# Agent attention and a maxout feed-forward in one kernel: the sum of exponentials folded on GpSimd at batch borders, with other orders around them and other engines for the last tiles

## Chip, cores and metric

The kernel runs on one core of a Trainium2 chip. Its time is the device time of one execution in microseconds; the time before is the median of six runs. Lower is better. The engines are named as in the profile: PE is TensorE (PEld its weight loads), DVE is VectorE, ACT is ScalarE, POOL is GpSimd, SP issues most of the DMAs.

## What is computed

There are 4 batches of 12544 tokens with 128 channels, 49 agents per batch, and a feed-forward with 768 hidden columns. Inputs and output are float32.

```python
def _attn_ref(q, k, v, agents):
    scale = 1.0 / np.sqrt(q.shape[-1])
    def sm(a, b):
        s = scale * (a @ b.transpose(0, 2, 1))
        s = s - s.max(-1, keepdims=True)
        e = np.exp(s)
        return e / (e.sum(-1, keepdims=True) + 1e-09)
    agent_v = sm(agents, k) @ v
    return sm(q, agents) @ agent_v

def _moe_ref(x, w1, w2, w3, w_out):
    h = np.maximum(np.maximum(x @ w1, x @ w2), x @ w3)
    return h @ w_out
```

The second function is applied to the rows that the first returns.

## The kernel before

**What it does with the algebra.** For each batch the 49 agents' values are formed from all of k and v. Their products with the differences w3-w1 and w2-w1 (and, for hidden block 4, with w3-w2) and with w1 @ w_out are kept in a tile G, one per batch. A token then needs only its 49 exponentials e: u = e·G(first difference), relu, v = e·G(second difference), a maximum, the product of the result with w_out, plus a linear term from G. The division by the sum of a token's exponentials comes last, on the output.

**Groups.** The tokens of q are worked off in 49 groups of 1024 (s = 0 to 48). Groups 0 to 11 are batch 0, 12 to 23 batch 1, 24 to 35 batch 2, 36 to 47 batch 3. Group 48 takes the last 256 tokens of each batch, so its u and v come in 8 matmuls of 128 columns instead of 2 of 512. A group has these steps; a step is named with its hidden block (0 to 5) or its half of the group (0 or 1), and with its group where that matters:

- qt, qe: q turned on PE (L651, 8 matmuls), copied to SBUF on DVE (L655). From group 36 on, and at groups 12, 24 and 36, a transposing DMA does this instead (L659).
- s, ex: scores (L665, 64-column matmuls) and exponentials e_q on ACT (L671).
- sum, rec: sums of the exponentials on PE (L676), their reciprocals on DVE (L682).
- u0 to u5, a0 to a5: first hidden product (L688, matmuls with 49 rows, two at a time) and relu on ACT (L703; block 4 in place, L700).
- v0 to v5, x0 to x5: second product (L688) and the maximum on DVE (L713; block 4 as a relu on ACT, L711). v4 adds onto the PSUM tile of u4, so it needs a4.
- lin0, lin1: linear term of each half (L718, 2 matmuls). oc00 to oc05, oc10 to oc15: output product of each half and block (L727, 4 matmuls of 128 columns each). sc0, sc1: division on DVE (L734). st: the output DMA on SP (L741).

u and v tiles (2 banks each) share a ring of three PSUM buffers; each is returned by its a or x (u4's by x4). Scores, sums, q's and the output halves share two single banks.

**The next batch beside it.** While the q groups of batch b-1 run, k and v of batch b are taken in 11 portions of 9 tiles of 128 rows (the last of 8), one per group: loads on SP, casts on POOL (L515, L519), k turned by a DMA (L523), scores ks (L366), exponentials ke on ACT (L371), values kv on PE (L535) and ka on DVE (L540). The step ea (L547, first portion L551) adds the exponentials of the first ten portions, 128x441 in float32, into Eacc on POOL.

**The border.** At groups 11, 23 and 35, `k_tail` (L565) finishes the next batch: reduce (red, L574) sums Eacc's nine blocks of 49 columns, total (tot, L579 and L581) adds over the partitions with a matmul with ones, and adds the last portion; normalise (nrm, L586 and L587) divides; p31, p21 (L506) multiply with the weight differences, and e31a, e31b on ACT and e21 on DVE put the product into G. The groups of the next batch read it.

**What sets the order.** Every step is put into a list with a key, 6 x (its group) + an offset (`at`, L247). The list is sorted by key and issued in that order; each engine works off its own steps in it. The offsets stand in tables: KEY (all plain groups), LATE (groups from 36 on, which have no k beside them), OWN (single groups), BORDER (two groups before a border to the second group after its start), HEAD, BATCH0 and BATCH3 (the border's own steps). `places` (L808) puts them together. The output DMAs are held back by up to 7 groups in the middle of the kernel.

**The end.** Group 48 writes four tiles of 256 rows: `end_scale` (DVE, L749) takes tiles 0 and 2, `end_scale_scalar` (ACT, L755, two activations each) tiles 1 and 3. Tiles 0 and 1 lie in the bank of output half 0, 2 and 3 in that of half 1. `end_store` (L757) issues tiles 0 and 2 from SP and 1 and 3 from ACT.

Of the kernel before, what the change touches and what calls it, by code (L numbers as in the profile page):

```python
# [9 lines left out]
FP32 = mybir.dt.float32  # L10
BF16 = mybir.dt.bfloat16
AF = mybir.ActivationFunctionType
ALU = mybir.AluOpType
# [15 lines left out]
    "s": -3.04749, "ex": -2.9048, "u1": -0.81512, "a1": -0.11576, "u2": 2.37421, "a2": 2.45765,  # L29
    "v1": 3.37564, "u3": 3.7004, "x1": 3.89334, "v2": 4.55864, "u0": 4.63, "a3": 4.65519, "x2": 4.7366,  # L30
    "a0": 5.00849, "v0": 5.38379, "u4": 5.77286, "x0": 6.25719, "a4": 6.54196, "u5": 7.04507,
    "v3": 7.1227, "x3": 7.44794, "v4": 7.51529, "lin1": 7.79655, "oc10": 8.14238, "sum": 8.14596,
    "rec": 8.17689, "oc12": 8.20379, "a5": 8.30536, "x4": 8.30648, "v5": 8.33752, "x5": 9.15285,
    "oc11": 9.49257, "oc13": 9.51825, "oc14": 10.09493, "lin0": 10.79959, "oc05": 10.84292,
    "oc15": 10.98413, "sc1": 11.49114, "oc02": 11.78965, "oc04": 11.82151, "oc00": 11.92155,
    "oc01": 12.02239, "oc03": 12.08397, "sc0": 12.87981, "st": 20.85007,
# [33 lines left out]
        "qt": -3.25348, "qe": -1.60938, "s": -1.08319, "ex": -0.07959, "ks": 0.24487, "ke": 0.69785,  # L70
        "u0": 0.71333, "a0": 1.42845, "v0": 1.46674, "u2": 1.55402, "ea": 1.95293, "u3": 2.01249,
        "sum": 2.04733, "kv": 2.10268, "a2": 2.26187, "a3": 2.44259, "u1": 3.00016, "x0": 3.08612,
        "v3": 3.16826, "rec": 3.3107, "ka": 3.48647, "a1": 4.24948, "x3": 4.28591, "v2": 4.7809,
        "u4": 4.96093, "x2": 5.54815, "a4": 6.34821, "u5": 6.35018, "a5": 6.53733, "v1": 6.53854,
        "v4": 6.56719, "x1": 6.7338, "x4": 6.84009, "v5": 6.91391, "x5": 6.9451, "lin1": 7.77018,
        "oc10": 8.3659, "lin0": 9.00035, "oc15": 9.04244, "oc04": 9.84141, "oc03": 10.06875,
        "oc01": 10.63146, "oc11": 10.91162, "oc00": 11.48787, "oc02": 11.69743, "oc05": 11.81297,
        "oc13": 11.92399, "sc0": 13.04207, "oc14": 13.24301, "oc12": 13.83351, "sc1": 15.27025,
        "st": 24.04256,
    },  # L80
    35: {
        "qt": -3.42697, "qe": -1.92735, "s": -1.33281, "ex": -1.31359, "ks": -0.92787, "sum": -0.87491,
        "ke": -0.36902, "kv": 0.32675, "ka": 0.59937, "rec": 0.88212, "u0": 0.88898, "a0": 0.90891,
        "v0": 1.17271, "u2": 1.45782, "a2": 2.00605, "u3": 2.51453, "x0": 2.59991, "v2": 2.93949,
        "a3": 3.20012, "u1": 3.23502, "a1": 3.44584, "x2": 3.51835, "v3": 3.942, "x3": 4.00627,
        "u5": 4.00643, "a5": 4.27302, "v5": 5.21895, "u4": 5.42122, "x5": 5.50884, "v1": 6.24909,
        "a4": 7.18659, "lin0": 7.89365, "oc03": 8.01405, "v4": 8.43263, "x1": 8.57785, "x4": 9.00519,
        "oc01": 9.40322, "oc02": 9.47513, "oc04": 10.01557, "oc00": 10.50745, "oc05": 10.70916,
        "lin1": 10.90156, "sc0": 11.20709, "oc15": 11.40347, "oc14": 11.51719, "oc11": 11.60961,
        "oc13": 13.16199, "oc12": 13.4014, "oc10": 13.57708, "sc1": 14.10054, "st": 28.07888,  # L90
    },
    36: {
        "s": -3.85762, "ex": -3.02118, "u1": -1.08192, "a1": 0.13487, "u2": 1.12084, "a2": 1.36634,
        "v2": 2.58017, "u0": 2.89822, "a0": 3.64302, "x2": 3.64864, "v1": 3.74492, "u3": 4.3491,
        "a3": 4.61245, "x1": 4.81452, "v0": 5.22302, "u4": 5.36733, "x0": 5.40904, "sum": 5.69395,
        "rec": 5.70943, "a4": 6.01497, "v3": 6.05388, "u5": 6.27145, "x3": 6.33451, "v4": 7.23655,
        "a5": 7.57697, "v5": 7.74872, "x4": 7.83644, "lin1": 7.8482, "oc10": 7.92453, "x5": 8.25933,
        "oc12": 8.53805, "oc14": 9.4705, "lin0": 10.11318, "oc00": 10.32008, "oc05": 11.08993,
        "oc11": 11.69579, "oc15": 11.95855, "oc13": 12.2097, "oc02": 12.27498, "sc1": 12.67367,
        "oc01": 13.63741, "oc04": 13.76201, "oc03": 14.31012, "sc0": 14.45082, "st": 20.04155,  # L100
    },
    37: {
        "s": -2.3763, "ex": -1.99168, "u1": -0.89023, "a1": -0.83864, "u2": 1.83631, "a2": 2.10039,
        "v2": 2.62074, "v1": 3.10251, "u0": 3.16911, "x2": 4.82079, "a0": 4.82575, "v0": 5.46426,
        "x1": 5.54152, "u3": 5.79276, "x0": 5.85326, "u5": 6.28625, "a3": 6.54158, "v3": 6.87889,
        "x3": 7.02476, "a5": 7.06215, "u4": 7.13124, "sum": 7.13155, "rec": 7.40011, "a4": 7.42192,
        "v5": 8.40138, "lin1": 8.44301, "x5": 8.50546, "oc11": 8.7139, "oc13": 8.85734, "v4": 9.11956,
        "oc10": 9.83416, "oc15": 9.91897, "lin0": 10.00468, "oc12": 10.1672, "x4": 10.46283,
        "oc02": 10.75773, "oc14": 10.97159, "oc01": 10.99548, "sc1": 11.08374, "oc05": 12.19635,
        "oc04": 12.41887, "oc00": 12.48727, "oc03": 12.57446, "sc0": 13.3308, "st": 13.63859,  # L110
    },
    47: {
        "s": -2.96572, "ex": -2.44054, "u1": -0.98286, "a1": -0.38292, "u0": 2.50098, "v1": 2.50777,
        "a0": 2.51445, "x1": 3.57249, "u2": 3.78871, "v0": 3.86021, "x0": 4.17982, "a2": 4.99948,
        "u3": 5.49603, "a3": 5.52978, "v2": 5.6013, "u4": 5.76145, "x2": 5.78978, "a4": 5.84387,
        "u5": 6.40472, "v4": 7.61729, "a5": 7.97742, "sum": 8.24781, "lin0": 8.29329, "oc00": 8.61937,
        "v3": 9.06308, "rec": 9.56376, "oc01": 10.03933, "x4": 10.07603, "x3": 10.6289, "v5": 10.86536,
        "lin1": 11.57727, "oc04": 11.9012, "oc14": 12.54349, "oc13": 13.40548, "x5": 13.64988,
        "oc02": 13.88884, "oc05": 14.16102, "oc03": 14.92264, "sc0": 16.27611, "oc12": 16.99023,
        "oc15": 17.06872, "oc11": 17.18888, "oc10": 17.27128, "sc1": 18.85812, "st": 23.913,  # L120
    },
    48: {
        "s": -3.4204, "ex": -2.49073, "u1": -1.6217, "a1": -0.87085, "v1": 0.78092, "x1": 2.62133,
        "u2": 4.49381, "a2": 4.991, "u0": 6.76262, "v2": 7.39248, "x2": 7.92987, "a0": 8.92021,
        "u5": 9.17989, "v0": 9.29415, "u4": 9.83418, "a5": 10.99894, "sum": 11.11918, "x0": 11.13319,
        "u3": 11.61847, "rec": 12.01294, "a4": 12.28323, "v5": 12.58725, "a3": 13.4554,
        "lin1": 13.86262, "oc10": 14.04021, "x5": 14.15402, "oc11": 14.85848, "v4": 16.25715,
        "x4": 17.85448, "v3": 19.03702, "lin0": 19.66535, "oc15": 20.01931, "oc01": 20.4512,
        "oc12": 22.46167, "x3": 24.03035, "oc05": 24.815, "oc14": 25.87451, "oc13": 26.8641,
        "sc1": 29.0489, "oc04": 29.05912, "oc03": 29.88451, "oc02": 30.80374, "sr1": 30.84707,  # L130
        "st2": 30.91835, "oc00": 43.00949, "st3": 43.44114, "sr0": 44.15505, "sc0": 47.77127,
        "st1": 53.21418, "st0": 99.95534,
# [3 lines left out]
    -2: {  # L136
        "qt": -3.12462, "qe": -2.07778, "s": -1.10921, "ex": -0.52776, "ks": -0.14113, "sum": 0.51396,
        "ke": 0.59984, "u0": 0.67536, "a0": 0.6961, "rec": 0.84156, "u2": 1.01073, "v0": 1.33353,
        "kv": 1.51787, "x0": 1.52149, "ea": 1.63837, "u3": 2.11923, "ka": 2.55578, "a2": 3.23616,
        "u1": 3.41714, "v3": 3.48808, "a3": 4.13748, "a1": 4.35524, "v2": 4.38204, "u4": 4.42344,  # L140
        "x3": 5.01917, "x2": 5.02462, "a4": 5.71198, "v4": 5.72872, "u5": 6.02153, "v1": 6.03887,
        "x1": 6.4518, "x4": 6.48251, "a5": 6.50269, "v5": 6.73587, "x5": 6.90186, "lin0": 8.02362,
        "oc03": 8.32254, "oc04": 9.0935, "oc02": 9.13616, "lin1": 9.64724, "oc14": 10.56583,
        "oc05": 11.74794, "oc00": 12.4679, "oc01": 12.97884, "sc0": 13.12636, "oc10": 13.12651,
        "oc13": 14.23702, "oc12": 14.3368, "oc15": 14.37162, "oc11": 14.51792, "sc1": 15.23195,
        "st": 23.00607,
    },
    -1: {
# [31 lines left out]
    },  # L180
}
BATCH0 = {
    "red": -0.90326, "tot": 0.17632, "nrm": 0.85576, "p31": 0.89274, "e31a": 0.96694, "p21": 1.05183,
    "e31b": 1.11618, "e21": 1.96962,
}
BATCH3 = {
# [6 lines left out]
def kernel(  # L193
# [53 lines left out]
    def at(key, fn):  # L247
        ops.append((key, len(ops), fn))
# [637 lines left out]
```

## Time and profile before

| | |
|---|---|
| median of 6 runs | 450.53 us (449.99 to 450.78) |
| the profiled execution | 449.99 us, span 448.2 us, granted clock 0.999 |
| a plain group, e.g. 14 to 19 | 8.15 us each |
| a late group, 38 to 45 | 7.71 us each |
| groups 9, 10, 11 (first border) | 9.66, 8.16, 8.40 us |
| groups 33 to 37 (third border) | 9.84, 8.66, 6.95, 7.29, 6.68 us |
| group 48 after group 47's end | 5.62 us to its last division, 2.7 us more to the end of the span |

The times of groups run from one group's sc1 end on DVE to the next one's. The profile gives busy time per engine, the chain of work that ended last, groups of equal instructions, and what ended an engine's idle time. A PE row's length is modelled: matmuls overlap, so the start of the next one tells more than its end. In a row of the timeline the first number is the start, the second the length in us; x6 means six instructions in one row, and brackets give the idle time before it and what ended it. In a row of busy times by stretch the columns are the stretch, its length, then PE, PEld, DVE, ACT and POOL busy time with instruction counts, the granted clock, the share of the DMA engines and GB/s.

### The profile page before, as it was taken

The numbers are of one execution on the slowest core, as the hardware profiler recorded it, in microseconds if no ns is written. First come the engines' busy times: TensorE is split into PE (matmuls) and PEld (weight loads), VectorE is DVE, ScalarE is ACT, GpSimd is POOL, SyncE is SP. The second block draws the span as 40 slices with busy tenths as digits, with TensorE's granted clock in tenths as the row PEclk, the third lists the DMA queues.
The fourth block names the chain that finished last, engine by engine and source line by source line (L and its number), as shares of the span: only waits on it lengthen the run. The fifth ranks groups of instructions, "written<-read, shape, count | busy, mean of one in ns | idle before, by whom it ended". The sixth has DMA issues, their size and how long they took to land.

```text
span 448.2 us, 13332 instructions
## 1 busy us (share of the span) xinstructions
PE 431.0 (96%) x5506; PEld 276.7 (62%) x5506; DVE 403.0 (90%) x506; ACT 399.1 (89%) x463; POOL 168.5 (38%) x164
## 2 busy tenths in 40 slices
PE   3898999999999999999999999999999999999995
PEld 2665566666665666666665766666655555565665
DVE  2335999999999999999999999999999999999995
ACT  1557999999989999999989999999989999999994
POOL 4432466565333544447513455545510111101000
PEclk9999999999999999999999999999999999999999
DMA  8999999898569999999999999997978686565932
GB/s 315 414 411 368 272 274 325 233 323 243 179 200 354 250 330 306 249 253 328 268 263 330 257 316 331 298 316 226 307 226 206 171 212 152 157 188 166 377 118 96
DMA packets 83800, 118.87 MB, mean 265 GB/s; under 512 B 57687, under 2 KB 59803, under 8 KB 83739
## 3 DMA queue, kind: packets, MB, share of 16 engines
q1 hardware_dynamic: 83248, 117.66, 86.5%
q8 instruction: 43, 0.70, 0.6%
q10 hardware_dynamic: 491, 0.36, 0.3%
q14 instruction: 18, 0.15, 0.1%
HBM read 78.74 MB, written 25.69 MB: 233 GB/s over the span
## 4 chain that ended last, share of the span: by engine, by line
PE 85%; DMA 8%; DVE 3%; ACT 2%; issue 1%; ACTq 0%; SPq 0%; DVEq 0%
PE uv_ps L688 34%; PE o_ps L727 32%; PE o_ps L718 6%; DMA st<-in_v_dram 5%; PE m_ps L665 3%; PE m_ps L651 3%; DVE r L713 2%; DMA st<-in_moe_w_dram 2%; PE m_ps L535 2%; PE m_ps L366 2%; ACT a_sb L703 1%; DMA ag_st<-in_agents_dram 1%; PE m_ps L676 1%; PE uv_ps L506 1%; DVE o_sb L734 0%
## 5 line engine op out<-in xcount | busy, mean ns | idle before, releaser
L713 DVE TENSOR_TENSOR r<-uv_ps,a_sb 128x1024 bf16<-128x1024 f32 x245 | 297.6, 1222 | 9.7 <-PE uv_ps L688 5.5
L703 ACT ACTIVATE a_sb<-uv_ps 128x1024 bf16<-128x1024 f32 x245 | 243.5, 1024 | 16.7 <-PE uv_ps L688 12.6
L688 PE MATMUL uv_ps<-e_q,G 49*128 49x512 bf16 (+1 forms) x1248 | 181.6, 369 | 1.6 <-ACT G L433 0.5
L727 PE MATMUL o_ps<-wo_bf,r 128*128 128x128 bf16 x2352 | 176.3, 220 | 0.0
L727 PEld LDWEIGHTS <-r 128*128 128x128 bf16 x2352 | 139.7, 98 | 42.0 <-issue 39.3
L688 PEld LDWEIGHTS <-G 49*128 49x128 bf16 x1248 | 57.0, 93 | 62.1 <-issue 23.0
L646 POOL CAST q_bf<-st 128x1024 bf16<-128x1024 f32 x49 | 51.0, 1040 | 95.7 <-DMA st<-in_q_dram 87.9
L734 DVE TENSOR_TENSOR o_sb<-o_ps,recips 128x512 f32<-128x512 f32 x96 | 65.8, 685 | 2.4 <-PE o_ps L727 0.8
L515 POOL CAST k_bf<-st 128x1152 bf16<-128x1152 f32 (+1 forms) x33 | 37.4, 1134 | 72.4 <-DMA st<-in_k_dram 72.4
L519 POOL CAST v_bf<-st 128x1152 bf16<-128x1152 f32 (+1 forms) x33 | 37.5, 1137 | 43.6 <-DMA st<-in_v_dram 38.3
L711 ACT ACTIVATE r<-uv_ps 128x1024 bf16<-128x1024 f32 x49 | 50.3, 1026 | 1.9 <-PE uv_ps L688 1.6
L700 ACT ACTIVATE uv_ps<-uv_ps 128x1024 f32<-128x1024 f32 x49 | 49.6, 1012 | 0.0
L718 PE MATMUL o_ps<-G,e_q 128*128 128x256 bf16 x196 | 38.0, 275 | 0.0
L547 POOL TENSOR_TENSOR Eacc<-Eacc,e_k 128x441 f32<-128x441 f32 x27 | 27.6, 1023 | 13.1 <-ACT e_k L371 10.2
L671 ACT ACTIVATE e_q<-m_ps 128x512 bf16<-128x512 f32 x49 | 29.2, 596 | 1.7 <-PE m_ps L665 0.8
L380 DVE COPY kT<-uv_ps 128x1152 bf16<-128x1152 bf16 (+1 forms) x11 | 8.3, 752 | 17.8 <-PE uv_ps L377 17.8
L718 PEld LDWEIGHTS <-e_q 128*128 128x128 bf16 x196 | 11.8, 97 | 20.0 <-issue 19.5
L655 DVE COPY qT<-m_ps 128x1024 bf16<-128x1024 bf16 x34 | 23.3, 686 | 0.4 <-PE m_ps L651 0.4
L651 PE MATMUL m_ps<-ident,q_bf 128*128 128x128 bf16 x272 | 21.3, 222 | 0.0
L665 PE MATMUL m_ps<-qT,agT 128*64 128x512 bf16 (+1 forms) x104 | 19.9, 389 | 0.0
L371 ACT ACTIVATE e_k<-m_ps 128x441 bf16<-128x441 f32 (+1 forms) x33 | 17.8, 539 | 2.1 <-PE m_ps L676 0.7
L651 PEld LDWEIGHTS <-q_bf 128*128 128x128 bf16 x272 | 16.5, 99 | 3.1 <-issue 2.1
(74 smaller groups left out, 219.9 us busy)
## 6 DMA issues: line engine op xcount, KB each, us to landing
st<-in_q_dram SPq DMA_DIRECT2D x48, 512.0 KB, 5.4
out_dram<-o_sb SPq DMA_DIRECT2D x48, 512.0 KB, 5.7
st<-in_k_dram SPq DMA_DIRECT2D x40, 576.0 KB, 5.3
st<-in_v_dram SPq DMA_DIRECT2D x40, 576.0 KB, 8.4
st<-in_k_dram SPq DMA_DIRECT2D x4, 512.0 KB, 5.3
st<-in_v_dram SPq DMA_DIRECT2D x4, 512.0 KB, 5.9
st<-in_moe_w_dram SPq DMA_DIRECT2D x2, 384.0 KB, 8.2
kT<-k_bf SPq DMA_TRANSPOSE x33, 4.0
```

The costliest lines, as they stand in the source:

```text
L515: nc.gpsimd.tensor_copy(out=d["kb"][:, :n, :], in_=d["k"][:, :n, :])
L519: nc.gpsimd.tensor_copy(out=d["vb"][:, :n, :], in_=d["v"][:, :n, :])
L646: nc.gpsimd.tensor_copy(out=d["qb"], in_=d["q"])
L651: nc.tensor.transpose(t[:, j * P:(j + 1) * P], d["qb"][:, j, :], ident)
L688: nc.tensor.matmul(t[:, h, j0 * P:j1 * P], G[b][h * H:h * H + A, col + f * P:col + (f + 1) * P], d["e"][h * H:h * H + A, j0 * P:j1 * P], s ...
L700: nc.scalar.activation(u, u, AF.Relu)
L703: nc.scalar.activation(a_sb[f], u, AF.Relu)
L711: nc.scalar.activation(r, v_ps[f], AF.Relu)
L713: nc.vector.tensor_tensor(out=r, in0=v_ps[f], in1=a_sb[f], op=ALU.max)
L718: nc.tensor.matmul(t[:, i * 2 * C:(i + 1) * 2 * C], d["e"][:, jj * P:(jj + 1) * P], G[batch[jj]][:, C1O:C1O + 2 * C], start=(i == 0), stop ...
L727: nc.tensor.matmul(t[:, c:c + C], r_sb[f][:, h, jj * P:(jj + 1) * P], wo_bf[:, f, :], start=False, stop=True, skip_group_check=True)
L734: nc.vector.tensor_tensor(out=d["out"][:, j:j + m, :], in0=d["o", o].rearrange("p (j c) -> p j c", c=C), in1=d["r"][:, j:j + m].unsqueeze( ...
```

## The change

1. The reduction leaves DVE. On POOL, four adds fold Eacc onto itself: blocks 5 to 8 onto 0 to 3 (196 columns), 3 and 4 onto 0 and 1 (98), 2 onto 1 (49), 1 onto 0 (49). The matmul with ones then reads Eacc's first 49 columns.
2. The tables LATE, BORDER, BATCH0, BATCH3 and the rows 34, 35, 36, 37, 47 and 48 of OWN get other offsets. KEY, HEAD and the rows for groups 0 and 1 stay.
3. In group 48 one engine takes both tiles of a half: DVE tiles 1 and 0, ACT tiles 2 and 3. Only tile 3 is stored from ACT, the others from SP.

```diff
         def reduce():
-            d["e"] = work.tile([P, A], FP32, tag="e_sum", name="e_sum")
-            nc.vector.tensor_reduce(out=d["e"], in_=Eacc[b].rearrange("p (j a) -> p a j", a=A),
-                                    axis=mybir.AxisListType.X, op=ALU.add)
+            e = Eacc[b]
+            m = KT
+            while m > 1:
+                h = m // 2
+                nc.gpsimd.tensor_tensor(out=e[:, :h * A], in0=e[:, :h * A], in1=e[:, (m - h) * A:m * A], op=ALU.add)
+                m -= h
 
         def total():
             out = host[s][:, ct:ct + A]
-            nc.tensor.matmul(out, ones, d["e"], start=False, stop=True, skip_group_check=True)
+            nc.tensor.matmul(out, ones, Eacc[b][:, :A], start=False, stop=True, skip_group_check=True)
...
-            (nc.scalar if i % 2 else nc.sync).dma_start(
+            (nc.scalar if i == 3 else nc.sync).dma_start(
...
-                at(key + K[f"sc{o}"], lambda o=o: end_scale(2 * o))
-                at(key + K[f"sr{o}"], lambda o=o: end_scale_scalar(2 * o + 1))
+                at(key + K[f"sc{o}"], lambda o=o: (end_scale_scalar if o else end_scale)(2 * o))
+                at(key + K[f"sr{o}"], lambda o=o: (end_scale_scalar if o else end_scale)(2 * o + 1))
...
 BATCH0 = {
-    "red": -0.90326, "tot": 0.17632, "nrm": 0.85576, "p31": 0.89274, "e31a": 0.96694, "p21": 1.05183,
-    "e31b": 1.11618, "e21": 1.96962,
+    "red": -1.03728, "tot": 0.4346, "nrm": 0.69166, "p31": 0.71682, "e31a": 1.03124, "p21": 1.72788,
+    "e31b": 1.87707, "e21": 2.33059,
 }
 BATCH3 = {
-    "red": -1.28697, "tot": 0.35013, "nrm": 0.77195, "p31": 0.91882, "e31a": 1.03104, "e31b": 1.44272,
-    "p21": 2.07801, "e21": 2.88209,
+    "red": -0.17478, "tot": 1.88239, "nrm": 3.65773, "p21": 4.07353, "e21": 4.85827, "p31": 5.01122,
+    "e31a": 5.49317, "e31b": 6.1648,
 }
```

The other tables only hold numbers. What they do to the order of PE's steps is shown here for the places of which the text speaks. One late group (40, with steps of its neighbours 39, 41 and 42), before and after:

```
u1.41 v0.40 u4.40 oc02.39 oc04.39 oc00.39 oc01.39 oc03.39 u5.40 v3.40 v4.40 lin1.40 oc10.40 sum.40 oc12.40
v5.40 u2.41 s.42 v1.41 oc11.40 oc13.40 u3.41 oc14.40 v2.41 u0.41 lin0.40 oc05.40 oc15.40

u1.41 v0.40 u4.40 oc01.39 oc05.39 oc02.39 oc04.39 sum.40 u5.40 v3.40 v4.40 lin1.40 oc10.40 oc11.40
v5.40 u2.41 s.42 v1.41 oc12.40 oc14.40 v2.41 u3.41 lin0.40 oc13.40 u0.41 oc15.40 oc00.40 oc03.40
```

In both, DVE works in the order sc1.39 x0.40 sc0.39 x3.40 rec.40 x5.40 x1.41 x2.41, and ACT in the order a1.41 a4.40 a5.40 x4.40 a2.41 ex.42 a3.41 a0.41. The first border from v0 of group 10 up to the products for G (the second is alike, 12 groups later):

```
v0.10 kv.10 u3.10 qt.11 u1.10 v3.10 lin0.9 oc02.9 s.11 v2.10 u4.10 oc03.9 oc00.9 oc04.9 ks.11 oc01.9 oc05.9
v4.10 u5.10 v1.10 kv.11 tot.11 sum.11 lin1.9 oc11.9 oc15.9 u0.11 v5.10 oc10.9 oc14.9 p31.11 oc12.9 oc13.9 p21.11

v0.10 u3.10 kv.10 qt.11 u1.10 v3.10 lin0.9 oc02.9 s.11 u4.10 v2.10 oc03.9 oc00.9 oc04.9 oc01.9 oc05.9 ks.11
v4.10 v1.10 u5.10 sum.11 kv.11 tot.11 lin1.9 oc11.9 oc15.9 v5.10 u0.11 p31.11 oc10.9 oc14.9 oc12.9 oc13.9 u2.11 p21.11
```

The third border is rearranged most: tot.35 is the 31st step after v4.33 before, and the 44th in the new order; p21.35 now comes before p31.35, which stands right ahead of v5.35 and u1.36, the first step that reads the new G. The last steps of PE:

```
... u3.48 v5.48 lin1.48 oc10.48 oc11.48 v4.48 v3.48 lin0.48 oc15.48 oc01.48 oc12.48 oc05.48 oc14.48 oc13.48
oc04.48 oc03.48 oc02.48 oc00.48

... v4.48 u5.48 v3.48 lin1.48 oc11.48 oc10.48 sum.48 v5.48 oc12.48 oc14.48 oc13.48 lin0.48 oc01.48 oc00.48
oc04.48 oc15.48 oc03.48 oc02.48 oc05.48
```

On POOL the fold stands behind the q cast of group 12, 24 or 36; at the third border the last ea stands behind that cast too. On SP, the output DMAs of groups 10 and 22 move about a group earlier, those of 12 and 24 two groups, those of 11 and 23 about four groups later, and those of 34 to 37 trade places; the k, v and q loads keep their order.

## The prediction on record

> **What bounds the kernel now.** I read the page's table of busy times first, then busy time by stretch, then single starts on the timeline. Groups are numbered by s; u3, v3, a3, x3, oc13, lin1, sc1, sum, tot are the steps named ahead of this text.
>
> ```profile
> PE 431.0 (96%) x5506; PEld 276.7 (62%) x5506; DVE 403.0 (90%) x506; ACT 399.1 (89%) x463; POOL 168.5 (38%) x164
> PE 85%; DMA 8%; DVE 3%; ACT 2%; issue 1%; ACTq 0%; SPq 0%; DVEq 0%
> ```
>
> TensorE is named as the bound. The stretches (one plain group, one with the first batch border, one late group; columns PE, PEld, DVE, ACT, POOL) show three engines nearly full:
>
> ```profile
> 100.36:108.51 8.15, 8.15 (x111) 5.36 (x110) 8.05 (x11) 7.75 (x10) 4.51 (x5) 1.00 0.85 265
> 124.74:134.40 9.66, 9.66 (x132) 6.14 (x128) 9.56 (x16) 8.60 (x11) 2.83 (x3) 1.00 0.75 228
> 378.90:386.61 7.71, 7.71 (x85) 4.48 (x84) 7.29 (x10) 7.43 (x9) 1.04 (x1) 1.00 0.68 170
> ```
>
> "PE 7.71 of 7.71" isn't all work: a matmul's end is modelled, so a wait hides inside a busy row. The spacing of starts shows it. Undisturbed, a 128-column matmul follows the last after 56 ns (an oc is 4, so 224), a u or v takes 216, lin 222, ks 228, kv 238, qt 457, sum 102, tot 447, p31 557. Where the form changes between 49-row, 64-column and full matmuls, each change adds 95 (151 for 56, 311 for 216). A plain group adds up to 8.00 of its 8.15; a late one, with 12 changes, to 7.22 of its 7.71. So the late groups lose 0.49 each. The rows show where:
>
> ```profile
> 378.82 1.22 DVE L713 TENSOR_TENSOR r<-uv_ps,a_sb 128x1024 bf16<-128x1024 f32 x1
> 379.72 0.11 PEld L688 LDWEIGHTS <-G 49*128 49x128 bf16 x3
> 380.08 0.09 PEld L688 LDWEIGHTS <-G 49*128 49x128 bf16 x1 [0.25 <-issue]
> ...
> 380.23 2.36 DVE L713 TENSOR_TENSOR r<-uv_ps,a_sb 128x1024 bf16<-128x1024 f32 x2
> ...
> 382.27 0.76 PE L688 MATMUL uv_ps<-e_q,G 49*128 49x512 bf16 x4
> 382.64 0.09 PEld L688 LDWEIGHTS <-G 49*128 49x128 bf16 x1 [0.26 <-issue]
> ```
>
> v5 starts at 379.73, u2 at 380.08: 354 for 216, because x3 (378.82, end 380.03) holds u2's PSUM buffer; u2 starts 52 ns after x3's end. u0 at 382.64 waits so for x1, v0 later for x2. Three prices follow: matmul start to ScalarE start 432, to VectorE start 502, engine end to matmul 52. With 1023 and 1220 for the operations, a buffer is back 1507 ns after its u began and 1774 after its v.
>
> **The fold.** Removed from VectorE, three times:
>
> ```profile
> L574 DVE TENSOR_REDUCE e_sum<-Eacc 128x49 f32<-128x441 f32 x3 | 2.8, 945 | 0.0
> L547 POOL TENSOR_TENSOR Eacc<-Eacc,e_k 128x441 f32<-128x441 f32 x27 | 27.6, 1023 | 13.1 <-ACT e_k L371 10.2
> ```
>
> 3 x 0.945 = 2.8 us of VectorE, but no PE wait over 30 ns stands between 124.7 and 134.4, so I count nothing for it directly; it only gives the new orders room. Added on GpSimd: adds of 196, 98, 49 and 49 columns, each needing the one before. From L547's row, 392/441 x 1023 = 0.9 if cost goes by columns. The casts (557 ns for 441 columns, 1040 for 1024) leave some 0.2 fixed, which gives about 1.5; with another 0.1 per dependence, 2.0. I take 1.5, range 0.9 to 2.0. A rule speaks against the move: the Trainium skill, GPSIMD Engine Reference, "Engine selection", sends two-input elementwise work and free-axis reductions to VectorE, GpSimd being about 2x slower. By the rule the change loses 0.6 to 1 us of engine time per border; by the rows GpSimd has it to spare:
>
> ```profile
> 124.52 1.04 POOL L646 CAST q_bf<-st 128x1024 bf16<-128x1024 f32 x1
> 131.23 1.15 POOL L515 CAST k_bf<-st 128x1152 bf16<-128x1152 f32 x1 [5.68 <-DMA st<-in_k_dram]
> ...
> 227.82 1.04 POOL L646 CAST q_bf<-st 128x1024 bf16<-128x1024 f32 x1 [3.44 <-DMA st<-in_q_dram]
> ```
>
> Behind the q cast the fold would run 125.6 to 127.1; tot, which reads it, starts at 130.09 (0.09 earlier in the new order): cover 4.4 us, cost nothing. At the second border the cast ends at 228.86 and tot starts at 229.57; a fold of 1.5 would hold PE 0.9 (bounds 0.3 to 1.5), and all of PE's queue with it. But that cast waited for its load behind two stores issued at 212.7; the new order issues two (of groups 10 and 12) one group earlier instead, so I expect the load some 2 us sooner, as at the first border, and count 0 with 1.5 kept for the range. The casts of the next k, queued behind the fold, wait for DMA anyway (5.68). At the third border the fold stands behind a q cast and an add, ready near 330.7; tot is moved 3.5 us later in PE's order: no cost. The other store moves only change when held tiles leave; each output buffer is still free over 9 places (some 12 us) before it is written again, so 0, at most 0.3 either way.
>
> **The orders.** PE's work hardly changes: 573 form changes before, 571 after. Here a rule counts: the Trainium skill, TensorEngine Tiling (Array Packing), "Key Properties", says that a change of tiling mode drains TensorE. The rows price it at 95 ns, so by the rule alone the orders are worth 2 x 0.095 = 0.2 us in all. The rows say waits are the larger store, so I went through each order for buffers and operands asked for sooner than 1507 or 1774 ns of undisturbed PE time after their producer:
> - First and second border, v0 of group 10 to u2 of group 15: 42.29 us, of it 41.24 work and 1.05 waits. Shortfalls sum to 0.98 in the old order (u5 after x3 of 11: 294; v5 after x1: 264), so the method fits; 0.71 in the new (v3 after x0 of 10: 248; u0 after x1 of 12: 184). Work falls 0.11. Gain 0.38 each, taken as 0.35 each (0 to 0.45).
> - Third border, v4 of 33 to the scores of 41: 52.3 us with 2.87 of waits, shortfalls 2.43 before and 1.53 after, work 0.1 less. Gain up to 1.0; taken as 0.8 because old waits exceed the shortfalls (-0.5 to 1.2).
> - Late groups, walked from v0 = 0 in the new order: u4 0.25, u5 1.64, v3 1.85; x0 starts at 0.50, its sc0 at 1.68, x3 so at 2.36, end 3.58; u2 may start at 3.63 instead of 3.37, the one big wait. v4 waits 0.14 for a4, which that wait absorbs. Then scores, v1, two oc, v2, u3, lin0, oc13, u0, three oc, u1 and v0 with nothing late: 7.55. x2 ends 0.2 before v0 needs it: the old loop had two x latencies, the new one. Gain 0.16 a group; five more groups 0.8 (0.2 to 1.5). What is late next is x3 with sc0 ahead of it.
> - Groups 46 and 47: my sum of waits is 1.1 in both orders. 0, -0.5 to 0.5.
>
> **The tail.** The end of the trace:
>
> ```profile
> 443.33 0.62 ACT L755 ACTIVATE o_end<-o_ps,recips 128x128 f32<-128x128 f32 x2 [1.17 <-DVE o_end L749]
> 443.99 0.38 ACTq L760 DMA_DIRECT2D out_dram<-o_end  x1
> 444.42 0.62 ACT L755 ACTIVATE o_end<-o_ps,recips 128x128 f32<-128x128 f32 x2 [0.46 <-ACT o_end L755]
> ...
> 445.07 0.42 DVE L749 TENSOR_TENSOR o_end<-o_ps,recips 128x256 f32<-128x256 f32 x1 [1.77 <-ACT o_end L755]
> ```
>
> The last oc starts at 443.34, so 4.86 us pass to the end at 448.2. The last tile is held up by the other pair, a DMA issue on ScalarE's queue, ScalarE's two activations, and only then VectorE. After: ScalarE scales both halves of the first tile while PE finishes the second; VectorE scales both halves of that one: 0.27 from matmul to VectorE, 0.36 + 0.42 for two, then the store, 2.70 from 445.50 to 448.2: 3.75. ScalarE's pair ends 0.3 sooner. Gain 1.1 (0.8 to 1.15, since three stores land close together).
>
> **Sum.** 0.7 + 0.8 + 0.8 + 0 + 1.1 = 3.4. The profiled execution took 449.99 with a span of 448.2, so it would be near 446.6; the median of six is 450.53, so I say 447.1.
>
> **Rivals.**
> - The late order gives nothing: a4's wait adds to x3's (7.22 + 0.14 + 0.26), and 0.1 of queueing makes the old 7.7. For it: ScalarE is busy 7.43 of 7.71. Against: the walk has v4's wait inside u2's. Without 0.8 and the third border's two late groups (0.3): 448.2.
> - The second border's q load comes no sooner and the fold is late there: +1.0, 448.1.
> - The change does only its tail, border waits moving from one buffer to another: 449.4.
> - Slower: each dependent GpSimd add costs over a microsecond, so that PE stands at tot at two borders. For a fold of F the loss is (F - 4.4) + (F - 0.6); from F = 4.65 on it eats the gain and 0.9 more. At F = 5.2 it is 5.4 - 3.4: 452.5. L547's 1.02 for 441 columns speaks against it.
>
> **Chances.** Forecast 0.62, late order 0.15, second border 0.11, tail alone 0.07, slower 0.05. A change of 0.2% (0.9 us) is about what a measurement of this kernel can tell, so faster is below 449.6: 0.88; same 0.07 (the tail-only case, at the edge); slower 0.05. The range 445.4 to 449.5 takes in the larger gains and the first three cases and leaves about 0.15 out.
>
> **What would show it.** Late groups at 7.55 instead of 7.71, with u2 held by x3 and v0 by nothing; four GpSimd adds summing to 1.5 us, ended before tot; group 9 to 11 together shorter than 26.2 by 0.35; 3.75 us from the last oc to the end. Wrong if late groups stay at 7.7, if PE stops ahead of tot, or if the last stores land late.

## The result, and the profile after

The changed kernel takes 448.74 us, median of 34 runs, against 450.68 us in 71 runs of the kernel before on the same chips: ratio 0.9958, 95% interval 0.9947 to 0.9970, a gain of 1.9 us where 3.4 were forecast. The forecast of 447.1 us was 1.6 us too low. The profiled execution took 448.98 us with a span of 447.2, against 449.99 and 448.2 before: only 1.0 us apart, since that execution of the kernel before lay 0.7 below its median and this one 0.2 above its own.

Lines of the changed kernel lie one lower than before up to the reduction and four lower behind it (L713 is now L717). The page's first lines:

```profile
span 447.2 us, 13333 instructions
PE 430.1 (96%) x5506; PEld 278.8 (62%) x5506; DVE 401.5 (90%) x503; ACT 396.4 (89%) x463; POOL 172.9 (39%) x176
```

VectorE has three instructions and 1.5 us less, GpSimd twelve instructions and 4.4 us more, and TensorE is busy 0.9 us less with as many matmuls. Busy time by stretch (a plain group; groups 9 and 21, which lead into the first and second border; late groups 40 and 41; columns as before):

```profile
101.04:109.18 8.14, 8.14 (x111) 5.35 (x110) 8.04 (x11) 7.74 (x10) 5.05 (x5) 1.00 0.82 261
125.42:135.71 10.29, 9.54 (x135) 6.17 (x133) 9.55 (x14) 8.81 (x12) 4.41 (x7) 1.00 0.80 231
225.53:235.06 9.53, 9.46 (x135) 6.17 (x133) 8.84 (x13) 8.57 (x12) 3.16 (x6) 1.00 0.73 206
379.23:387.11 7.88, 7.59 (x84) 4.67 (x82) 7.18 (x9) 7.21 (x9) 1.04 (x1) 1.00 0.76 171
387.11:394.63 7.52, 7.52 (x84) 4.58 (x82) 7.18 (x9) 7.20 (x9) 1.04 (x1) 1.00 0.64 175
```

The late group went from 7.71 to 7.52, near the walked 7.55. Group 21 went from 9.65 to 9.53. Two things were not forecast: group 9 is longer than before, 10.29 for 9.66, with PE idle for 0.75 of it, and one late group, 40, takes 7.88 with PE idle for 0.29.

From single starts, in the two profiled executions (us):

| stretch | before | after | change | forecast |
|---|---|---|---|---|
| start of the span to u0 of group 0 | 41.15 | 41.81 | +0.66 | 0 |
| first border, v0 of 10 to u2 of 15 | 42.29 | 42.90 | +0.61 | -0.35 |
| second border, v0 of 22 to u2 of 27 | 42.27 | 42.16 | -0.11 | -0.35 |
| third border, v4 of 33 to scores of 41 | 52.32 | 51.68 | -0.64 | -0.8 |
| scores of 41 to v0 of 46 | 49.91 | 49.19 | -0.72 | -0.8 |
| v0 of 46 to the last oc | 20.74 | 20.55 | -0.19 | 0 |
| last oc to the end | 4.86 | 4.23 | -0.63 | -1.1 |

Their sum is -1.0, the difference of the spans. The first line isn't the change's: its code is the same, and in the eleven further traces below it lies anywhere from 41.1 to 41.9. Without it the sum is -1.7, near the -1.9 of the medians. So 1.7 us of the forecast are missing: 1.2 at the first two borders, 0.5 in the tail, and small change elsewhere.

What fills the hole at the first border stands in the timeline (start, length, engine and line, operation):

```profile
126.19 1.70 POOL L578 TENSOR_TENSOR Eacc<-Eacc 128x196 f32<-128x196 f32 x4
...
131.76 0.46 DVE L590 RECIPROCAL k_recip<-m_ps 128x49 f32<-128x49 f32 x1
132.09 1.14 POOL L516 CAST k_bf<-st 128x1152 bf16<-128x1152 f32 x1 [4.21 <-DMA st<-in_k_dram]
132.26 1.04 DVE L591 TENSOR_TENSOR avT<-Vacc,k_recip 128x49 bf16<-128x49 f32 x1
133.36 0.62 PE L507 MATMUL uv_ps<-wall,avT 128*64 128x512 bf16 x6 [0.68 <-DVE avT L591]
```

The fold, first row, is over 2.9 us before the matmul that reads it (L583, 130.86) and harms nothing. But `normalise`, two operations of 49 columns on VectorE, ends late: its multiply takes 1.04 us, and PE waits 0.68 at p31. The row above it is the cast of the next k on GpSimd: the multiply starts 0.17 after the cast and ends 70 ns after it. Before, the same multiply took 0.47 at this border, beside the cast of 131.23, and 0.21 at the two others:

```profile
131.98 0.47 DVE L587 TENSOR_TENSOR avT<-Vacc,k_recip 128x49 bf16<-128x49 f32 x1
```

In the changed kernel it is long at the third border as well: 0.63, beside a cast of q.

### The profile page after: what moved, and what is told of

Read it like the earlier page. It is cut to its first block, busy times and chain, and to the rows that moved or that the text cites. A ratio compares the mean times of both kernels' runs of the same rounds, so it can differ in the third digit from the quotient of the medians.

```text
span 447.2 us, 13333 instructions
## 1 busy us (share of the span) xinstructions
PE 430.1 (96%) x5506; PEld 278.8 (62%) x5506; DVE 401.5 (90%) x503; ACT 396.4 (89%) x463; POOL 172.9 (39%) x176
## 4 chain that ended last, share of the span: by engine, by line
PE 82%; DMA 9%; DVE 4%; ACT 3%; issue 1%; DVEq 0%; SPq 0%; ACTq 0%
PE uv_ps L692 33%; PE o_ps L731 31%; PE o_ps L722 6%; DMA st<-in_v_dram 5%; PE m_ps L669 3%; PE m_ps L655 3%; DVE r L717 3%; DMA st<-in_moe_w_dram 2%; PE m_ps L536 2%; ACT a_sb L707 2%; PE m_ps L367 2%; DMA ag_st<-in_agents_dram 1%; PE m_ps L680 1%; PE uv_ps L507 1%; DVE o_sb L738 1%
## 5 line engine op out<-in xcount | busy, mean ns | idle before, releaser
L717 DVE TENSOR_TENSOR r<-uv_ps,a_sb 128x1024 bf16<-128x1024 f32 x245 | 296.8, 1223 | 10.6 <-PE uv_ps L692 4.5
L731 PE MATMUL o_ps<-wo_bf,r 128*128 128x128 bf16 x2352 | 173.9, 220 | 0.0
L516 POOL CAST k_bf<-st 128x1152 bf16<-128x1152 f32 (+1 forms) x33 | 37.4, 1134 | 61.7 <-DMA st<-in_k_dram 61.7
L391 POOL CAST k_bf<-st 128x1152 bf16<-128x1152 f32 (+1 forms) x11 | 12.5, 1137 | 16.2 <-DMA st<-in_k_dram 14.1
```

Source lines behind the costliest of these rows:

```text
L516: nc.gpsimd.tensor_copy(out=d["kb"][:, :n, :], in_=d["k"][:, :n, :])
L717: nc.vector.tensor_tensor(out=r, in0=v_ps[f], in1=a_sb[f], op=ALU.max)
L731: nc.tensor.matmul(t[:, c:c + C], r_sb[f][:, h, jj * P:(jj + 1) * P], wo_bf[:, f, :], start=False, stop=True, skip_group_check=True)
```

## The experiments

My first theory was that the multiply of Vacc by the reciprocals, with both operands in SBUF, stands still while a GpSimd cast works on SBUF, and that the new order brings the two closer together. The rivals were that the new order itself is late there, or that the fold on GpSimd is at fault. For the borders as a whole the question was what the orders are worth without this. For the tail: whether the three output stores from one queue, or three transfers at once, cost the missing time.

**The same kernel again**, to see what repeats.

> The changed kernel once more, for a second trace of it. Theory A (the first trace was unlucky by its slow head and by the 0.35 us event in group 40; the border's avT multiply, with both inputs in SBUF, is stretched from 0.21 to about 1 us whenever a GpSimd cast runs beside it): late groups 7.53 again, head and group 40 back to the old values or changed at random, and the first border (v0 of group 10 to u2 of 15) at 42.2 if avT is not hit there, 42.9 if it is. Rival B (the new order itself costs 0.6 at the first border): 42.9 there again with avT at 0.2 us. Ratio to the kernel before 0.995 to 0.997.

> The changed kernel a third time, as the measure for the two versions beside it. All theories: 1.7 to 2.2 us below the kernel before; first border 42.9 with avT stretched, late group 40 at 7.88.

They gave 448.94 us (0.9972, 0.9956 to 0.9987) and 448.17 us (0.9928, 0.9898 to 0.9958). The first border took 42.91 and 43.06 against the 42.90 above, with the multiply at 1.04 and 1.20; group 40 took 7.88 in both. So neither is a chance of one execution. The second of them lies 2.6 us below the kernel before, more than the 1.7 to 2.2 expected. The three ratios of this one kernel, 0.9928 to 0.9972, show how far a set of runs moves a ratio, so the small edits below are read from their traces.

**The fold alone, in the old orders.**

```diff
-            d["e"] = work.tile([P, A], FP32, tag="e_sum", name="e_sum")
-            nc.vector.tensor_reduce(out=d["e"], in_=Eacc[b].rearrange("p (j a) -> p a j", a=A),
...
+            while m > 1:
+                h = m // 2
+                nc.gpsimd.tensor_tensor(out=e[:, :h * A], in0=e[:, :h * A], in1=e[:, (m - h) * A:m * A], op=ALU.add)
+                m -= h
...
```

> The kernel before with the fold on GpSimd alone, old orders, old tail. Theory A: first and third border unchanged; at the second the fold stands behind a q cast that ends 0.7 us before tot, so PE waits there 0.5 to 1.0 us; VectorE's 0.945 us is not turned into time anywhere; total +0.3 to +1.0 us. Rival B (VectorE's freed time is what the change lives from): each border 0.3 to 0.8 shorter, total -1 to -2 us.

451.18 us, ratio 1.0019 (1.0002 to 1.0036): no gain, rather a small loss. The first two borders took 42.33 and 42.35, as before. The third took 45.62 to the scores of 40, 1.0 more than the kernel before. So the place I had named for a late fold, the second border, was the wrong one. The timeline at the third:

```profile
327.08 1.04 POOL L649 CAST q_bf<-st 128x1024 bf16<-128x1024 f32 x1 [2.19 <-DMA st<-in_q_dram]
328.08 1.70 POOL L577 TENSOR_TENSOR Eacc<-Eacc 128x196 f32<-128x196 f32 x4
329.83 0.30 PEld L582 LDWEIGHTS m_ps<-Eacc,ones 128*128 128x128 f32 x2 [0.94 <-POOL Eacc L577]
329.84 0.42 PE L582 MATMUL m_ps<-Eacc,ones 128*128 128x49 f32 x2 [0.83 <-POOL Eacc L577]
```

The fold stands behind a q cast that waits for its load, and PE stands at tot for the fold. This is what a late fold looks like, and it shows what the new order of the third border does: it moves tot later in PE's order, so that in the changed kernel tot waits 0.05 there.

**The new orders with the reduction left on VectorE.** The same edit the other way, on the changed kernel.

> The changed kernel with the reduction back on VectorE, new orders and new tail kept. Theory A (the orders and the tail are the gain, the fold only makes room): late groups 7.53 and tail as in the changed kernel; borders 0 to 0.5 longer each, total 0 to 1.5 us above the changed kernel, still below the kernel before. Rival B (the fold is the gain): back near 450.5.

449.58 us, ratio 0.9985 (0.9958 to 1.0012). The first border took 42.82 in the trace, so the fold isn't what makes it long. The second took 42.78 against 42.16 with the fold: groups 21 and 23 were each 0.3 longer. In group 21, u5 of 22 waits 0.22 for x2, which VectorE reaches late because the reduction stands ahead of it. Group 23's loss isn't the fold's: x3 of group 24 starts 0.35 late behind nothing that the trace shows, a gap of the kind that the last experiments of this section are about. So the fold is worth some 0.3 there, not 0.6. The granted clock fell to 0.88 in the stretch from 325.82 to 337.02 of this trace, so the third border isn't read from it. Neither the fold nor the orders give the whole gain alone.

**The multiply without a second operand in SBUF.** The reciprocals are written back where they come from, in PSUM.

```diff
-            r = work.tile([P, A], FP32, tag="k_recip", name="k_recip")
-            nc.vector.reciprocal(r, host[s][:, ct:ct + A])
+            r = host[s][:, ct:ct + A]
+            nc.vector.reciprocal(r, r)
             nc.vector.tensor_tensor(out=avT[b % 2][:, :A], in0=Vacc[b], in1=r, op=ALU.mult)
```

> The changed kernel with the border's reciprocal left in PSUM, so that the avT multiply has one input in SBUF and one in PSUM. Theory A: avT takes 0.2 to 0.3 us at all three borders whatever GpSimd does, and no wait ahead of p31 over 0.1 us stands at the first border: 42.2 there, total 0.3 to 0.8 us below the changed kernel. Rival B (avT waits for something else than a shared way into SBUF): avT is still near 1 us where a GpSimd cast runs beside it.

The timeline at the first border, this kernel:

```profile
131.94 0.48 DVE L590 RECIPROCAL m_ps<-m_ps 128x49 f32<-128x49 f32 x1
...
132.22 1.14 POOL L516 CAST k_bf<-st 128x1152 bf16<-128x1152 f32 x1 [4.28 <-DMA st<-in_k_dram]
132.46 0.21 DVE L591 TENSOR_TENSOR avT<-Vacc,m_ps 128x49 bf16<-128x49 f32 x1
...
132.72 0.63 PE L507 MATMUL uv_ps<-wall,avT 128*64 128x512 bf16 x6
```

The cast runs beside the multiply exactly as it did, and the multiply takes 0.21 us. Its three calls took 0.209 to 0.211. The first border fell from 42.90 to 42.21; the second was 42.22. That settles the cause of the first border's loss: not the fold, and not waits that the order makes for PE, but this operation's two SBUF operands beside a GpSimd cast. The orders only set how early in the cast the multiply starts. The kernel took 448.24 us, ratio 0.9959 (0.9939 to 0.9979). The two ratios don't tell it from the changed kernel; the trace does.

**The tail alone, on the kernel before.**

```diff
-            (nc.scalar if i % 2 else nc.sync).dma_start(
+            (nc.scalar if i == 3 else nc.sync).dma_start(
...
-                at(key + K[f"sc{o}"], lambda o=o: end_scale(2 * o))
-                at(key + K[f"sr{o}"], lambda o=o: end_scale_scalar(2 * o + 1))
+                at(key + K[f"sc{o}"], lambda o=o: (end_scale_scalar if o else end_scale)(2 * o))
+                at(key + K[f"sr{o}"], lambda o=o: (end_scale_scalar if o else end_scale)(2 * o + 1))
```

> The kernel before with the new choice of engines for group 48's tiles and stores alone (old orders, reduction on VectorE). Theory A (the chain of scalings after the last output matmul is shortened by 1.0, and 0.35 of it is given back because three stores land together): last oc to last scaling 1.1 to 1.2 instead of 2.15, from there to the end 3.0 instead of 2.7; total -0.6. Rival B (the tail needs the new order of group 48 as well, since the old one finishes half 1 and half 0 in another way): less than 0.3 gained.

449.99 us, ratio 0.9988 (0.9973 to 1.0003). From the last oc to the last division it took 1.18 us (2.15 before, 1.18 in the changed kernel), from there to the end 3.01 (2.71 and 3.05). So the tail's gain is its own, 0.7 here, and part of what the divisions gain is lost with the stores.

**One of the three stores back on ScalarE's queue**, on top of the reciprocals in PSUM.

```diff
-            (nc.scalar if i == 3 else nc.sync).dma_start(
+            (nc.scalar if i % 2 else nc.sync).dma_start(
```

> The changed kernel with the reciprocal in PSUM and tile 1 stored from ScalarE again, as before the change. Theory A (the last store lands 0.34 later than before because it stands in SP's queue right behind tile 1's): from the last scaling to the end 2.7 instead of 3.04, total -0.3 against the version with tile 1 on SP. Rival B (the stores share the DMA engines, whichever queue they come from): 3.0 stays.

The last division to the end took 3.19, not less than 3.05. (With the engines of the changed kernel for tiles and stores it lay between 3.01 and 3.16 in nine traces.) Moving one store to the other queue moves the hold-up with it: ScalarE's second issue now starts 0.22 after the last division. The kernel took 448.18 us, 0.9947 (0.9921 to 0.9974), no different from the one it was made from. Of the 0.34 that the end lost, 0.09 is the last issue on SP, which starts 0.12 instead of 0.03 after the last division, behind tile 1's; the other 0.25 is its landing, 1.97 us after that issue instead of 1.72, with the three other stores issued in the 0.9 us before it. That they hold each other up at the DMA engines is argued; the times are measured.

**The late groups' table alone.**

```diff
 LATE = {
-    "s": -3.04749, "ex": -2.9048, "u1": -0.81512, "a1": -0.11576, "u2": 2.37421, "a2": 2.45765,
+    "s": -2.9742, "ex": -2.69831, "u1": -0.20723, "a1": 0.3452, "u2": 2.54405, "a2": 2.67071,
...
```

> The kernel before with the new LATE offsets alone, used from group 38 to 46. Theory A: 7.53 per late group instead of 7.71, with the one repeated wait at v4 (for a4) of 0.15 and no wait of u2 or v0 over 0.06; with eight groups -1.4 before the ends, total -0.8 to -1.5 as the old row of group 47 meets the new ones. Rival B (the late groups gain from what comes before them): 7.71 stays.

453.16 us, ratio 1.0051 (1.0024 to 1.0077): slower, and the expectation missed. The groups inside the loop took 7.53 as they do in the changed kernel. The loss is at the seams to groups that keep their old tables: group 36 took 7.99 (7.29 before), 45 took 9.20 (7.71), 46 took 8.41 (7.62), 37 took 7.30 (6.68). A table of offsets is worth its price only with the tables of its neighbours; which buffer is late at each seam I did not trace.

**Group 40: does its 0.35 belong to the order?** All late groups from 38 to 45 have the same order, yet only 40 is long. The timeline of the changed kernel there (v5 on PE, the reciprocal, then x5 on VectorE, and PE's next u, which waits for it):

```profile
379.88 1.02 ACT L715 ACTIVATE r<-uv_ps 128x1024 bf16<-128x1024 f32 x1
...
380.19 0.63 PE L692 MATMUL uv_ps<-e_q,G 49*128 49x512 bf16 x4
380.30 0.20 DVE L686 RECIPROCAL recips<-m_ps 128x8 f32<-128x8 f32 x1
...
381.05 2.36 DVE L717 TENSOR_TENSOR r<-uv_ps,a_sb 128x1024 bf16<-128x1024 f32 x2 [0.55 <-ACT r L715]
...
382.32 0.39 PE L692 MATMUL uv_ps<-e_q,G 49*128 49x512 bf16 x2 [0.28 <-DVE r L717]
```

v5 starts at 380.19, so x5 should start 0.50 later, at 380.69; it starts at 381.05. The bracket names ScalarE's x4, which ended at 380.90, but x5 doesn't need it, as the last trace of this section shows. If this gap depends on where the instruction lies in VectorE's program, a few instructions put ahead of everything must move it. Three more fills of a tile of ones at VectorE's start, on top of the reciprocals in PSUM:

```diff
     nc.vector.memset(ones_bf, 1.0)
+    nc.vector.memset(ones_bf, 1.0)
+    nc.vector.memset(ones_bf, 1.0)
+    nc.vector.memset(ones_bf, 1.0)
```

> The changed kernel with the reciprocal in PSUM and three idle memsets put at VectorE's start, which shifts VectorE's code by three instructions. In three traces with the fold, x5 of group 40 starts 0.36 us late, behind nothing that the trace shows; without the fold (three VectorE instructions more) it did not. Theory A (it is where VectorE's code has to be loaded): group 40 is 7.53 as its neighbours, total -0.3 against the version without memsets. Rival B (it comes from the order or the stores there): 7.88 stays.

> Reciprocal in PSUM and three idle memsets on VectorE, timed with more rounds. Theory (avT's stretching costs 0.7 at the first border and 0.2 at the third, the code's place 0.36 at group 40, of which it gives back 0.2 net elsewhere): 0.8 to 1.3 us below the changed kernel, 2.6 to 3.2 below the kernel before. If the two causes were only in the traces: no difference from the changed kernel beyond 0.3 us.

447.72 and 447.73 us, ratios 0.9925 (0.9898 to 0.9952) and 0.9923 (0.9895 to 0.9951). Group 40 took 7.53 in both. The event didn't vanish: group 15 now took 8.50 instead of 8.15 in both, and group 30, 8.46 in the kernel without the fills, took 8.15. (Group 32 took 8.49 in one of the two only.) The second of them is 0.4 us below the changed kernel timed beside it (448.17) and 3.0 below the kernel before, where 0.8 to 1.3 and 2.6 to 3.2 were expected. With eight fills instead of three:

> The same with eight memsets. Theory (a late instruction of 0.36 us appears where VectorE's code has to be loaded at a moment without slack, so it moves with the code): plain groups 15 to 22 or late group 40 change by 0 or 0.36 each against the version with three, nothing else changes. Rival (three memsets removed the event for good): the same trace as with three.

446.96 us, ratio 0.9895 (0.9859 to 0.9931), the lowest of all. Its interval overlaps that of the changed kernel timed beside it (0.9898 to 0.9958), but five of its six executions took 446.7 to 447.0 us, and all eight of the changed kernel 448.0 or more. Its timeline at the same place of group 40:

```profile
377.93 1.02 ACT L723 ACTIVATE r<-uv_ps 128x1024 bf16<-128x1024 f32 x1
...
378.25 0.63 PE L700 MATMUL uv_ps<-e_q,G 49*128 49x512 bf16 x4
378.35 0.20 DVE L694 RECIPROCAL recips<-m_ps 128x8 f32<-128x8 f32 x1
...
378.75 2.36 DVE L725 TENSOR_TENSOR r<-uv_ps,a_sb 128x1024 bf16<-128x1024 f32 x2 [0.20 <-PE uv_ps L700]
```

x5 starts 0.50 after v5, as it should, and while ScalarE's x4 is still at work (377.93 to 378.95), so it doesn't wait for that; the releaser in the bracket before was only the last event that the page could see. Groups 15, 30 and 40 took 8.15, 8.15 and 7.53. The eight fills cost nothing visible, as VectorE waits for loads at the start.

So the event goes with VectorE's place in its program, and the thirteen traces show which places. Number VectorE's instructions in a trace from 0, those that wait for semaphores included. Every gap of 0.34 to 0.41 us ahead of a maximum (x of groups 0 to 47) that neither its v, nor its a, nor VectorE's own work explains stands at number 63, 319, 447, 575 or 703. There are 27 such gaps, and each place is 63 plus a multiple of 128. Other instructions at these places have at most 0.14 us of idle time before them. That the engine is loading instructions there is argued: a packet of 8192 bytes on q14, a queue that the page lists as "instruction", starts 0.7 to 3.8 us after each of them, but it isn't shown to be VectorE's. The kernel before has such an event too, in group 30 (8.52 where 8.15 stands in the kernel with the fold alone).

The spans of the kernel with the reciprocals in PSUM (446.4) and of this one (444.9) differ by 1.5 us: 0.7 in groups 30, 31 and 40, and 0.8 ahead of group 1, in the stretch that varies by itself.

## Why the prediction was right, and where it was wrong

**The total: right in direction, a little over half in size.** 1.9 us of the 3.4 came. By itself 448.74 would speak rather for two of the rivals (448.1 and 448.2) than for the forecast; the stretches show that neither of them happened. Of the third rival (449.4) one half did: at the first two borders the waits moved from one buffer to another.

**What bounds it: right.** The waits hidden in TensorE's busy time were where the time was, and the price list (432, 502, 52, 95 ns) carried over to the new trace.

**The fold's own cost: right.** Forecast 1.5 us, measured 532 + 394 + 2 x 268 = 1.46, and 1.70 from the first add's start to the last one's end; that is 1.5 to 1.8 times the 0.945 on VectorE. The groups of equal instructions (busy in all, mean ns):

```profile
L578 POOL TENSOR_TENSOR Eacc<-Eacc 128x49 f32<-128x49 f32 x6 | 1.6, 268 | 0.5
L578 POOL TENSOR_TENSOR Eacc<-Eacc 128x196 f32<-128x196 f32 x3 | 1.6, 532 | 0.1
L578 POOL TENSOR_TENSOR Eacc<-Eacc 128x98 f32<-128x98 f32 x3 | 1.2, 394 | 0.2
```

The fixed part of about 0.2 that I took from the casts was right, and none of the six adds of 49 columns came near a microsecond, so the slower rival fell. "It only gives the new orders room" held: alone it gave nothing, and without it the second border lost some 0.3.

**The second border's load: right.** I expected it "some 2 us sooner". Its cast began at 227.05 instead of 227.82, only 0.8 sooner from the start of the span; but PE came to this border 1.3 later (v0 of group 22 at 224.96 instead of 223.66), so that the cast was 2.1 sooner against PE's work. The fold ended at 229.75, 1.2 ahead of tot, which started at 230.97.

**The first two borders: wrong, and this is the step that failed.** I wrote: "Shortfalls sum to 0.98 in the old order (u5 after x3 of 11: 294; v5 after x1: 264), so the method fits; 0.71 in the new". The sum fitted by chance. In the trace of before those two shortfalls are one wait of 0.26 at u5 of group 11, for x3. Two products in a row (four matmuls) take 0.61 where nothing waits, and 0.87 there:

```profile
136.81 0.61 PE L688 MATMUL uv_ps<-e_q,G 49*128 49x512 bf16 x4
...
138.34 0.87 PE L688 MATMUL uv_ps<-e_q,G 49*128 49x512 bf16 x4
```

The other 0.8 of the 1.05 is many gaps of 10 to 30 ns, which plain groups have as well (0.15 each) and which no order removes. In the new order the two shortfalls that I named came out as 0.24 (v3 of 10) and 0.16 (u0 behind x1 of 12). So waits went from 1.05 to 1.08 where nothing else disturbed them, in the kernel with the reciprocals in PSUM, and the stretch from 42.29 to 42.21: -0.08 instead of -0.35. The second border, -0.11, says the same. Two shortfalls of one chain must not be added, and a sum that agrees must be checked by place.

**What I did not see at all** was the multiply of `normalise`. It added 0.7 at the first border and 0.24 at the third. The row was there in the trace of before: L587's mean of 299 ns over three is 215, 215 and 467, and the 467 one lay beside the k cast of 131.23. I weighed what GpSimd could take from TensorE and not what it could take from VectorE. The Trainium skill, GPSIMD Engine Reference, "Key points", says that GpSimd shares its SBUF interfaces with VectorE and contends with instructions that read two SBUF inputs. The runs agree and give its size: up to 1.20 us for 0.21. The loss isn't the new orders' alone: in two versions with the old orders at this border (the tail alone, the late table alone) the multiply took 0.69 and 0.75 and the border 42.50 and 42.57. Against these the changed kernel is 0.3 to 0.4 longer there, not 0.61; the trace of before, with 0.47, is a mild case.

**The third border: right.** 0.8 forecast, 0.64 measured (0.44 to the scores of 40, 0.20 in the late group behind them). That includes a loss that I didn't see, the multiply beside a cast of q: with the reciprocals in PSUM the stretch took 51.44, so the order itself gave 0.88. The reason given, "old waits exceed the shortfalls", was weak, since the first two borders show what such an excess is made of; that the number came close is in part luck.

**The late groups: right in size, half right in place.** 7.55 forecast, 7.53 measured, so the rival that the order gives nothing fell. But the wait that I put at u2 (0.26, with v4's 0.14 inside it) is one of 0.15 at v4 for a4; no other is over 0.05. The stretch gained 0.72 and not more because 0.35 went to the event in group 40.

**Groups 46 to 48:** 0 forecast, 0.19 gained.

**The tail: the mechanism right, a term mis-sized.** Last oc to last division: 2.15 before, 1.05 by the walk, 1.18 measured; the walk's 0.27 from matmul to VectorE runs from the last of the oc's four matmuls, and from the first, where the stretch begins, it is 0.43. I then took "the store, 2.70", the duration of before, though I had written that three stores land close together. It measured 3.05. The timeline of the end, in the changed kernel:

```profile
442.72 1.14 ACT L759 ACTIVATE o_end<-o_ps,recips 128x128 f32<-128x128 f32 x4 [1.75 <-PE o_ps L731]
...
443.37 1.31 SPq L764 DMA_DIRECT2D out_dram<-o_end  x3
443.39 0.76 DVE L753 TENSOR_TENSOR o_end<-o_ps,recips 128x256 f32<-128x256 f32 x2 [1.16 <-PE o_ps L731]
443.89 0.39 ACTq L764 DMA_DIRECT2D out_dram<-o_end  x1
```

Each pair of tiles is scaled by one engine without a pause, as the walk had it. The last division ends at 444.15 and the span at 447.2. All four stores are issued between 443.37 and 444.7, where before the held-up divisions spread them. The gain was 0.63 of 1.1.

**Open:** why the start of the span varies by 0.8 us between traces, what VectorE does in the gaps at its instructions 63 + 128n, and which buffers are late at the seams of the late table alone.

## What to carry to other kernels

Before adding up the waits that an order will remove, find each of them in the trace by its place: shortfalls along one chain are one wait, and gaps of 10 to 30 ns per matmul are no store to draw on. When work moves in time or to another engine, look at which operations it will newly run beside, small ones ahead of a matmul first; one operand read from PSUM instead of SBUF took 0.7 us off the path here. Where an engine starts late and nothing explains it, count its place in the engine's program before blaming the order. A table of offsets for one part of a pipeline is measured with its neighbours' tables, never alone.

## What the runs showed of the hardware

- A VectorE multiply of 128x49 with both operands in SBUF does not share with a GpSimd cast but waits it out. It took 0.21 us without a cast beside it and, started beside one, between 0.47 and 1.20 us in ten cases of different runs and borders, longer the earlier in the cast it began, ending 62 to 68 ns after the cast each time. Started 0.18 us ahead of the cast (second border, reduction on VectorE) it took 0.21. With one operand in PSUM it took 0.21 beside the same casts.
- Single gaps of 0.34 to 0.41 us on VectorE stand in fixed groups of a kernel and move to others when 3 or 8 instructions are put at its start (group 40 and 30, then 15, then none of these). All 27 in thirteen traces stand at VectorE's instruction 63 plus a multiple of 128. The two in groups 30 and 40 together are 0.7 us, as much as most edits here are worth.
- Last stores that are issued closer together ended later: 3.05 us from the last division to the end instead of 2.71, of which 0.25 is the last store's landing (1.97 us after its issue instead of 1.72), and no less with two stores on each of two queues (3.19).
